# A fused attention and MLP kernel: first weight chunk in fp32, one tiled stretch per batch, second attention moved into the first MLP

## The chip, the core and the metric

The kernel runs on one core of one Trainium2 chip. The metric is device time in microseconds (us) of one execution. Every time below is from runs at a mean granted TensorE clock of 0.98 to 1.00, unless said otherwise. Engines: PE is TensorE (matmuls), PEld its weight loads, DVE is VectorE, ACT is ScalarE, POOL is GpSimd, SP is SyncE, which here only issues DMAs.

## The reference, cut to what matters

```python
# x: [8, 8, 512, 64] (batch, head, token, d); state: [8, 8, 32, 64]
xread = softmax(x @ state.T / 8) @ state        # 512 rows of a head
sread = softmax(state @ x.T / 8) @ x            # 32 rows of a head
y = concat([xread, sread], axis=2)              # heads are laid side by side: [8*544, 512]
out = silu(y @ w_in) @ w_out                    # w_in [512, 2048], w_out [2048, 512]
```

The kernel never forms `xread`. For each batch it multiplies the state into `w_in` first and calls the result `W1` (256 x 2048); then `silu(a @ W1) @ w_out` is the MLP of that batch's 512 xread rows, with `a` the normalised attention. The sread rows of all batches make one last small MLP.

## The kernel before

Work of PE, per batch: `g1(b, ft)` is two matmuls of 128x512 and a SILU on ACT, for 16 values of ft; `g2(b, tt, ft)` is one matmul of 128x512, 64 of them. I call these 96 matmuls per batch the wide ones. PE further does the transposes `x_T`, `a_T`, the scores `sc`, the tiled matmuls `w1_m` that make W1, and the tiled `sread_m`.

```python
def w1_m(b, j, bks):                     # W1, one chunk of 512 columns: 8 matmuls in 8 tiles of the array
    for kt in range(KT):
        for half in range(2):
            nc.tensor.matmul(bank[bks[half]][ds(32 * kt, 32), :],
                sbd[ds(64 * half, 64), b, kt, half, :],
                w_in_sb[ds(64 * half, 64), kt, ds(512 * j, 512)],
                ..., tile_position=(64 * half, 32 * kt))

def g1(b, ft):
    bk = bank[f"h{hctr[0] % 2}"]         # only two banks, h0 and h1, in turn
    ...                                  # two matmuls W1 x aT into bk
    nc.scalar.activation(g[b % 2][:, ft, :], bk[:], func=SILU, bias=0.0)

def att_tail(fill, b, s, a0, sg, dg):    # a phase: 64 g2 matmuls of batch k, with work of batch k+1 filled in
    add(fill, s, L(exs, b), L(W1p, b, 0))                       # W1 chunks 0 and 1
    ...
    add(fill, s + 14, L(W1p, b, 1), L(sread_m, b, "a1"), L(sread_n, b, "a1"))   # chunks 2 and 3, sread
    ...
    for i in range(16):
        add(fill, sg + dg * i, L(g1, b, i))
```

(Cuts are marked with dots.) The start loads x of batch 0 and of batch 1 on SP's queue, does the attention of both, and only then makes the first W1 chunk and starts the first MLP; `warm` matmuls on zeros fill PE's gaps meanwhile (the granted clock was 1.00). The first MLP runs both batches' `g1` steps interleaved with batch 0's `g2` steps, four `g2` at a time (`G2`), while the weights still arrive in eight chunks, `wi` and `wo` 0 to 3. The kernel uses PSUM as eight banks of 128x512 fp32, named o0, o1, w0, w1, h0, h1, a0, a1.

The softmax here doesn't subtract the row's maximum and nothing guards it: scores larger than these inputs give would overflow.

Of the kernel before, what the change touches and what calls it, by code (L numbers as in the profile page):

```python
# [19 lines left out]
def kernel(  # L20
# [8 lines left out]
    nc = tc.nc  # L29
# [13 lines left out]
    st_f = [pers.tile([128, 128], FP32, name=f"st_f{i}") for i in range(2)]  # L43
    st_nat = pers.tile([128, B, 128], BF16, name="st_nat")
# [81 lines left out]

    def x_T(b, kt, bk):
        v = bf(bk).rearrange("p (k c t) -> p k c t", k=2, c=4)
        for c in range(4):
            nc.tensor.transpose(  # L130
                v[:, kt % 2, c, :], x_n[b % 2][:, kt, c, ds(2, 128)], ident[:]
            )
# [14 lines left out]
    def x_Td(b):  # L147
        nc.sync.dma_start_transpose(
            xT[b % 2][:].rearrange("p k c t -> p (k c) t"),
            x_u[:].rearrange("p k c h d -> p (k c h d)"),  # L150
        )
        nc.vector.tensor_copy(
            x_n[b % 2][:, :, :, ds(2, 128)].rearrange("p k c e -> p (k c) e"),
            x_u[:].rearrange("p k c h d -> p (k c) (h d)"),
        )
# [28 lines left out]
    def norm_m(b, eng, kt=0, n=4):  # L184
        e = nc.vector if eng == "dve" else nc.gpsimd
        e.tensor_tensor(  # L186
            an[b % 2][:, :, :, ds(kt, n), :].rearrange("p h c k s -> p (h c) k s"),
            en[b % 2][:, :, :, ds(kt, n), :].rearrange("p h c k s -> p (h c) k s"),
            rs[b % 2][:, :, :, ds(kt, n)]
            .rearrange("p h c k -> p (h c) k")  # L190
            .unsqueeze(3)
            .to_broadcast([128, 8, n, NS]),
            op=MULT,
        )
# [53 lines left out]
    def w1_m(b, j, bks):  # L248
        for kt in range(KT):
            for half in range(2):  # L250
                nc.tensor.matmul(  # L251
                    bank[bks[half]][ds(32 * kt, 32), :],
                    sbd[ds(64 * half, 64), b, kt, half, :],
                    w_in_sb[ds(64 * half, 64), kt, ds(512 * j, 512)],
                    start=True,
                    stop=True,
                    skip_group_check=True,
                    tile_position=(64 * half, 32 * kt),
                )
# [66 lines left out]
    with tc.manual_schedule():  # L326
# [4 lines left out]
        for kt in range(KT):  # L331
            if kt == 2:
                nc.sync.dma_start(st_f[1][:], state[1].rearrange("h ns d -> ns h d"))
            load_x(1, nc.sync, kt, 1)
# [4 lines left out]
        make_identity(nc, ident[:])  # L339
# [7 lines left out]
        OB = XB  # L347
# [11 lines left out]
        def exs(b):  # L359
            for q in range(2):  # L360
                ex(b, 2 * q, 2, AB[q])
# [6 lines left out]
        cast_x(0, "dve", (0,))  # L368
        cp("pool", st_nat[:, 0, :], st_f[0][:])
        x_T(0, 0, XB[0])  # L370
        x_Te(0, 0, 1, XB[0], "act")
        cast_x(0, "dve", (1,))
        st_T(0, "a1", "act", "dve")
        cast_x(0, "dve", (2,), (0,))
        cast_x(0, "pool", (2,), (1,))
        cast_x(0, "dve", (3,), (0,))
        cast_x(0, "pool", (3,), (1,))
        cast_x(1, "pool", (0,), (1,))
        load_wi(0)
        load_wo(0)  # L380
        warm(8, "w1")
        x_T(0, 1, XB[1])
        x_Te(0, 1, 1, XB[1], "act")
        sc(0, 0, SB[0])
# [3 lines left out]
        x_Te(0, 2, 1, XB[2], "act")  # L388
        sc(0, 1, SB[1])
        ex(0, 1, 1, SB[1])  # L390
        warm(3, "w1")
        x_T(0, 3, XB[3])
        cast_x(1, "dve", (0,), (0,))
        x_Te(0, 3, 1, XB[3], "dve")
        warm(3, "o0")
# [3 lines left out]
        cast_x(1, "dve", (1,))  # L399
        cast_x(1, "act", (2,))  # L400
        norm_s(0, 0, 2)
        norm_m(0, "pool", 0, 2)
        x_T(1, 0, "o0")
        x_T(1, 1, "o0")
        x_Te(1, 0, 2, "o0", "dve")
        cp("act", st_nat[:, 1, :], st_f[1][:])
        cast_x(1, "act", (3,))
        warm(8, "a0")
        st_T(1, "a1", "dve", "dve")
        norm_s(0, 2, 2)  # L410
        norm_m(0, "pool", 2, 2)
        x_T(1, 2, "o1")
        x_T(1, 3, "o1")
        x_Te(1, 2, 2, "o1", "act")
        warm(4, "a0")
        sc(1, 0, "w0")
        sc(1, 1, "w0")
        ex(1, 0, 2, "w0")
        warm(8, "a0")
        sc(1, 2, "w1")  # L420
        sc(1, 3, "w1")
        ex(1, 2, 2, "w1")
        nc.scalar.preload_act_table(SILU)
        warm(8, "a0")
        a_T(0, (("a0", "dve"), ("a1", "dve")))
        W1x(0, 0, ("o0", "o1"), DA)
        load_wi(1)
        load_wo(1)
        load_wi(2)
        load_wo(2)  # L430
        norm_s(1, 0, 2)
# [3 lines left out]
        warm(6, "o0")  # L435


        g1(0, 0)
        g1(0, 1)
        sread_m(0, "a0")  # L440
        sread_n(0, "a0")
        g1(0, 2)
        g1(0, 3)
        load_wi(3)
        load_wo(3)
        load_x(2, nc.gpsimd)
        for b in range(2, B):
            load_st(b)
        G2(0, 0)
        sread_t(0, "a0", "dve")  # L450
        sread_m(1, "a1")
        sread_n(1, "a1")
        G2(0, 1)
        sread_t(1, "a1", "dve")
        a_T(1, (("a0", "dve"),))
        G2(0, 2)
        W1x(0, 1, AB, DA)
        G2(0, 3)
        W1x(1, 0, AB, DA)
        for j in (1, 2, 3):  # L460
            n = 3 * j - 3
            g1(0, 4 * j)
            g1(1, n)
            W1x(1, j, AB, DA)
            g1(0, 4 * j + 1)
            g1(0, 4 * j + 2)
            G2(0, 4 * j)
            g1(0, 4 * j + 3)
            G2(0, 4 * j + 1)
            g1(1, n + 1)  # L470
            if j == 3:
                cast_xu(2, "dve", (0, 1))
                cast_xu(2, "pool", (2, 3))
                x_Td(2)
                st_T(2, "a0", "dve", "dve")
            G2(0, 4 * j + 2)
            if j < 3:
                W1x(0, j + 1, AB, DA)
            g1(1, n + 2)
            G2(0, 4 * j + 3)  # L480
# [3 lines left out]
        g1(1, 9)  # L484


        WP = (("w0", "w1"), ("h0", "h1"))

        def W1p(b, i):
            for j in range(2):  # L490
                w1_m(b, 2 * i + j, WP[j])
            for j in range(2):
                w1_e(b, 2 * i + j, WP[j], DD if j == 0 else ("act", "act"))

        def phase(k, fill):
            for tt in range(4):
                bk = ("o0", "o1")[tt % 2]
                for ft in range(16):
                    g2(k, tt, ft, bk)
                    for f in fill.get(16 * tt + ft, ()):  # L500
                        f()
                o_e(k, tt, bk)

        def add(fill, step, *fs):
            fill.setdefault(int(step), []).extend(fs)
# [4 lines left out]
        def att_head(fill, b, s0, s1):  # L510
            add(fill, s0, L(st_T, b, "a0", "dve", "dve"))
            add(fill, s0, L(x_Td, b))
            if 4 < b + 1 < B:
                add(fill, s0, L(load_x, b + 1, nc.sync))
            add(fill, s1, L(scs, b, 0))
            add(fill, s1 + 2, L(scs, b, 1))

        def att_tail(fill, b, s, a0, sg, dg):
            add(fill, s, L(exs, b), L(W1p, b, 0))
            add(fill, s, L(norm_s, b, 0, 2), L(norm_m, b, "pool", 0, 2))  # L520
            add(fill, s, L(norm_s, b, 2, 2), L(norm_m, b, "dve", 2, 2))
            add(fill, s, L(nc.scalar.preload_act_table, SILU))
            add(fill, s + 14, L(W1p, b, 1), L(sread_m, b, "a1"), L(sread_n, b, "a1"))
            if b == 2:
                add(fill, a0, L(a_T, b, (("a0", "act"),)))
            else:
                add(fill, s, L(a_Td, b))
            add(fill, a0 + 2, L(sread_t, b, "a1", "dve"))
            for i in range(16):
                add(fill, sg + dg * i, L(g1, b, i))  # L530

        fill = {}
        for i in range(10, 16):
            add(fill, i - 10, L(g1, 1, i))
        add(fill, 2, L(scs, 2, 0))
        add(fill, 3, L(scs, 2, 1))
        att_tail(fill, 2, 6, 30, 35, 1.8)
        add(fill, 6, L(cast_xu, 3), L(load_x, 4, nc.sync))
        att_head(fill, 3, 37, 58)
        phase(1, fill)  # L540

        for k in range(2, 7):
            fill = {}
            att_tail(fill, k + 1, 0, 24, 35, 1.8)
            if k + 2 < B:
                add(fill, 0, L(cast_xu, k + 2))
                att_head(fill, k + 2, 34, 56)
            phase(k, fill)


        fill = {}
        for i in range(16):
            add(fill, 2 + 3 * i, L(g1, 8, i))
        phase(7, fill)
# [5 lines left out]
        for i, cols in enumerate(((0, 256), (256, 512))):  # L560
            for ft in range(16):
                g2(8, 1, ft, ("o1", "w0")[i], cols)
            o_e(8, 1, ("o1", "w0")[i], "dve" if i else "act", nc.sync if i else nc.scalar, cols)
# [30 lines left out]
```

## Time and profile before

| | before |
|---|---|
| time, median of the first 3 runs | 221.55 us (221.09 to 221.85) |
| span of the profiled run | 219.7 us |
| PE busy | 209.2 us, 95% |
| first wide matmul | 15.89 us in the records, in fact 15.68 (below) |
| one phase in the middle | 23.15 us |

From the page of the kernel before: busy time and share of the span of each engine, the row of PE in 40 slices (in tenths), and the chain of waits by engine.

```profile
PE 209.2 (95%) x1652; PEld 104.2 (47%) x1678; DVE 84.0 (38%) x171; ACT 131.5 (60%) x221; POOL 40.7 (19%) x78
PE   7779999999999999999999999999999999999993
...
PE 90%; DMA 2%; SPq 2%; issue 1%; ACT 1%; DVE 1%; POOL 0%
```

PE bounds the kernel, except in the first three slices. The timeline of PE, kernel before, shows the end of that start (columns: start, length, engine, line, operation, tiles, shapes, count, idle time before and what ended it).

```profile
12.67 0.61 PE L321 MATMUL ps_a<-zeros 128*128 128x128 bf16 x8
13.50 0.62 PE L202 MATMUL ps_a<-ident,an 128*128 128x128 bf16 x8 [0.22 <-POOL an L186]
14.05 0.41 PE L251 MATMUL ps_o<-w_in_sb,sbd 64*32 64x512 bf16 x8
15.34 0.49 PE L321 MATMUL ps_o<-zeros 128*128 128x128 bf16 x6 [0.88 <-DVE W L79]
15.89 0.81 PE L272 MATMUL ps_h<-aT,W 128*128 128x512 bf16 x3
```

The transposes of the attention wait for POOL's normalisation, then come the first W1 group (L251), its eviction by DVE, and the first `g1`. A record is missing here: `g1(0, 0)` and `g1(0, 1)` are four wide matmuls, and the view has three. The trace has the weight loads of all four, the first at 15.62, when the last of the six `warm` matmuls starts (they are 0.055 us apart), so the first wide matmul was at about 15.68. The run e8b_old_start (below), which has the same start and no record missing here, shows four, the first 0.06 us after the last `warm`:

```profile
15.78 0.49 PE L323 MATMUL ps_o<-zeros 128*128 128x128 bf16 x6 [0.88 <-DVE W L79]
16.11 1.03 PE L274 MATMUL ps_h<-aT,W 128*128 128x512 bf16 x4
```

The next lines, from the view of the kernel before, are one phase's two tiled stretches.

```profile
95.75 0.59 PE L296 MATMUL ps_o<-w_out_sb,g 128*128 128x512 bf16 x2
96.28 0.41 PE L251 MATMUL ps_w<-w_in_sb,sbd 64*32 64x512 bf16 x8
96.50 0.56 PE L251 MATMUL ps_h<-w_in_sb,sbd 64*32 64x512 bf16 x8
97.23 2.97 PE L296 MATMUL ps_o<-w_out_sb,g 128*128 128x512 bf16 x13 [0.16 <-issue]
100.13 0.41 PE L251 MATMUL ps_w<-w_in_sb,sbd 64*32 64x512 bf16 x8
100.35 0.40 PE L251 MATMUL ps_h<-w_in_sb,sbd 64*32 64x512 bf16 x8
100.68 0.43 PE L218 MATMUL ps_a<-x_n,en 128*32 128x65 bf16 x32
101.27 2.54 PE L296 MATMUL ps_o<-w_out_sb,g 128*128 128x512 bf16 x11 [0.16 <-issue]
```

Two things have to be known to read this. Wide matmuls start 0.216 us apart when nothing holds them, though each is shown with 0.38 us: they are pipelined. (The Trainium skill, "TensorE: Matmul & The Clock Gate", Back-to-back issue gap, gives N / 2.4 + 2.5 ns for a single warm matmul, which is 0.216 us for 512 columns; this trace has it. The same section puts a sustained stream of such matmuls, each with its weight load, at about 0.131 us; this trace does not agree, since its streams of them keep 0.216, and the measurement decides.) And the program has 14 wide matmuls between the two stretches where the trace has 13: the one right after a stretch is missing in the records, which is what "idle 0.16" stands for. So the first stretch lasts from 96.18 (95.75 and two matmuls) to 97.02, 0.84 us, and the second from 100.03 to 101.05, 1.02 us.

### The profile page before, as it was taken

Reading aid. Unit: us, or ns where it says so; the run is one execution under the profiler, and the core shown is the slowest. Engines: PE = TensorE matmul, PEld = TensorE weight load, DVE = VectorE, ACT = ScalarE, POOL = GpSimd, SP = SyncE. Lnnn points to the kernel's source line nnn. Section 1 sums busy time; section 2 is a strip of 40 time slices with the busy share of each in tenths; the row PEclk is TensorE's granted clock in tenths of the full one; section 3 lists DMA queues with packets and bytes.
Section 4 is the critical chain, followed back from the end, with each engine's and each line's share of the span. In section 5 each row is a group of like instructions: output and inputs, shape, how many; then the busy total and the mean of one; then the engine's idle time right before and its main releaser. Section 6 shows DMA issues by size and latency. Waiting matters only on the chain.

```text
span 219.7 us, 4129 instructions
## 1 busy us (share of the span) xinstructions
PE 209.2 (95%) x1652; PEld 104.2 (47%) x1678; DVE 84.0 (38%) x171; ACT 131.5 (60%) x221; POOL 40.7 (19%) x78
## 2 busy tenths in 40 slices
PE   7779999999999999999999999999999999999993
PEld 7555334453544444444444444444443444566552
DVE  4767321445730672139312841087107600111110
ACT  3873766669677846776477837692669277433210
POOL 1778222001600070007000610043001000000000
PEclk9999999999999999999999999999999999999999
DMA  6899999289551138512770269015411311111112
GB/s 204 229 179 169 206 232 188 42 225 286 191 120 51 48 97 189 196 48 51 187 243 3 69 169 276 16 51 145 95 48 51 97 48 51 49 48 48 51 48 96
DMA packets 36868, 26.56 MB, mean 121 GB/s; under 512 B 20848, under 2 KB 32368, under 8 KB 36848
## 3 DMA queue, kind: packets, MB, share of 16 engines
q1 hardware_dynamic: 30160, 20.39, 32.8%
q0 software_dynamic: 6128, 5.44, 14.8%
q10 hardware_dynamic: 560, 0.46, 0.6%
q8 instruction: 13, 0.21, 0.4%
q14 instruction: 7, 0.06, 0.1%
HBM read 17.30 MB, written 8.91 MB: 119 GB/s over the span
## 4 chain that ended last, share of the span: by engine, by line
PE 90%; DMA 2%; SPq 2%; issue 1%; ACT 1%; DVE 1%; POOL 0%
PE ps_o L296 49%; PE ps_h L272 25%; PE ps_w L296 4%; PE ps_h L283 3%; DMA x_f<-in_x_dram 2%; PE ps_w L251 2%; PE ps_h L251 2%; PE ps_a L218 1%; SPq L91 1%; PE ps_a L160 1%; PE ps_a L251 1%; ACT x_n L83 1%; PE ps_a L202 1%; DVE W L79 1%; POOL an L186 0%
## 5 line engine op out<-in xcount | busy, mean ns | idle before, releaser
L296 PE MATMUL ps_o<-w_out_sb,g 128*128 128x512 bf16 x462 | 124.8, 379 | 2.3 <-issue 1.7
L280 ACT ACTIVATE g<-ps_h 128x512 bf16<-128x512 f32 x128 | 75.7, 598 | 51.9 <-PE ps_h L272 49.6
L272 PE MATMUL ps_h<-aT,W 128*128 128x512 bf16 x248 | 73.6, 379 | 0.5 <-DVE W L79 0.3
L296 PEld LDWEIGHTS <-g 128*128 128x128 bf16 x512 | 47.9, 98 | 51.8 <-issue 1.6
L79 DVE COPY o_sb<-ps_o 128x512 f32<-128x512 f32 x30 | 20.6, 689 | 91.7 <-PE ps_o L296 76.7
L272 PEld LDWEIGHTS <-W 128*128 128x128 bf16 x256 | 24.3, 98 | 29.7 <-issue 1.6
L186 POOL TENSOR_TENSOR an<-en,rs 128x512 bf16<-128x512 bf16 x9 | 9.5, 1060 | 110.8 <-ACT W L83 56.6
L81 POOL CAST x_u<-x_f 128x256 bf16<-128x256 f32 x44 | 17.8, 447 | 4.5 <-DMA x_f<-in_x_dram 4.5
L79 DVE CAST W<-ps_w 128x512 bf16<-128x512 f32 x24 | 15.3, 679 | 3.5 <-PE ps_w L251 3.5
L83 ACT ACTIVATE W<-ps_h 128x512 bf16<-128x512 f32 x24 | 13.1, 603 | 0.1
L291 ACT ACTIVATE g_s<-ps_h 128x256 bf16<-128x256 f32 x16 | 6.1, 383 | 11.2 <-PE ps_h L283 11.2
L181 DVE TENSOR_REDUCE rs<-en 128x16 f32<-128x512 bf16 x16 | 10.5, 659 | 3.2 <-ACT en L171 3.1
L79 DVE CAST W<-ps_a 128x512 bf16<-128x512 f32 x7 | 4.8, 691 | 14.2 <-PE ps_a L251 14.2
L283 PE MATMUL ps_h<-xsT,w_in_sb 128*128 128x256 bf16 x64 | 9.6, 273 | 0.0
L296 PE MATMUL ps_w<-w_out_sb,g 128*128 128x512 bf16 x32 | 9.5, 379 | 0.1
L283 PEld LDWEIGHTS <-w_in_sb 128*128 128x128 bf16 x64 | 6.3, 98 | 4.1
L160 PEld LDWEIGHTS <-xT 128*128 128x128 bf16 x128 | 5.9, 98 | 4.3 <-DVE xT L79 0.4
L251 PEld LDWEIGHTS <-sbd 64*32 64x32 bf16 x256 | 3.1, 88 | 9.9 <-issue 9.4
L508 ACT ACT_TABLE_LOAD x6 | 7.7, 1283 | 0.1
L171 ACT ACT_TABLE_LOAD x6 | 7.7, 1283 | 0.1
L321 PEld LDWEIGHTS <-zeros 128*128 128x128 bf16 x86 | 6.6, 116 | 2.3 <-DVE zeros L335 1.2
L171 ACT ACTIVATE en<-ps_a 128x512 bf16<-128x512 f32 (+1 forms) x14 | 7.3, 564 | 0.4 <-PE ps_a L160 0.2
(66 smaller groups left out, 126.7 us busy)
## 6 DMA issues: line engine op xcount, KB each, us to landing
out_dram<-o_sb SPq DMA_DIRECT2D x32, 256.0 KB, 2.3
x_f<-in_x_dram SPq DMA_DIRECT2D x5, 1024.0 KB, 6.7
x_f<-in_x_dram SPq DMA_DIRECT2D x8, 256.0 KB, 4.5
w_in_sb<-in_moe_w_in_dram POOLq DMA_DIRECT2D x4, 512.0 KB, 9.6
w_out_sb<-in_moe_w_out_dram POOLq DMA_DIRECT2D x4, 512.0 KB, 11.9
x_f<-in_x_dram POOLq DMA_DIRECT2D x1, 1024.0 KB, 18.1
out_dram<-o_sb ACTq DMA_DIRECT2D x1, 256.0 KB, 2.5
st_nat<-in_state_dram POOLq DMA_DIRECT2D x6, 32.0 KB, 13.1
```

The source lines that it names most:

```text
L79: nc.vector.tensor_copy(dst, src)
L81: nc.gpsimd.tensor_copy(dst, src)
L83: nc.scalar.activation(dst, src, func=COPY, bias=0.0)
L160: nc.tensor.matmul(v[:, kt % 2, :, c, :], xT[b % 2][:, kt, c, :], sbd[:, b, kt, :, :], start=True, stop=True, skip_group_check=True,)
L171: nc.scalar.activation(en[b % 2][:, :, :, ds(kt, n), :].rearrange("p h c k s -> p k (h c) s"), v[:, ds(kt % 2, n)], func=EXP, bias=0.0, sc ...
L181: nc.vector.tensor_reduce(v, en[b % 2][:, :, :, ds(kt, n), :], axis=AX, op=ADD)
L186: e.tensor_tensor(an[b % 2][:, :, :, ds(kt, n), :].rearrange("p h c k s -> p (h c) k s"), en[b % 2][:, :, :, ds(kt, n), :].rearrange("p h ...
L251: nc.tensor.matmul(bank[bks[half]][ds(32 * kt, 32), :], sbd[ds(64 * half, 64), b, kt, half, :], w_in_sb[ds(64 * half, 64), kt, ds(512 * j, ...
L272: nc.tensor.matmul(bk[:], W1[b % 2][:, half, ds(128 * ft, 128)], aT[b % 2][:, half, :, :], start=(half == 0), stop=(half == 1), skip_group ...
L280: nc.scalar.activation(g[b % 2][:, ft, :], bk[:], func=SILU, bias=0.0)
L283: nc.tensor.matmul(bk[:, 0:256], w_in_sb[:, kt, ds(128 * ft, 128)], xsT[:, kt, :, :, :], start=(kt == 0), stop=(kt == KT - 1), skip_group_ ...
L296: nc.tensor.matmul(bank[bk][:, c0:c1], src[:, ft, ds(128 * tt, 128)], w_out_sb[:, ft, c0:c1], start=(ft == 0), stop=(ft == 15), skip_group ...
```

## The change

The intent is to start the first MLP earlier and to leave tiled mode less often. The first W1 chunk's `w_in` columns come uncast, on SP's queue right behind batch 0's x, and are multiplied in fp32, so that the chunk need not wait for POOL's casting queue. Batch 1's load and attention move out of the start into the first MLP. In the phases, all four W1 groups of a batch and its sread come in one tiled stretch. The core of the diff, cut:

```diff
+    def st_f32(bk, e0, e1): ...          # the state of batch 0, in fp32
+    w_f = x_f[1][:].rearrange("p k h e -> p k (h e)")
+    def w1f_m(bks): ...                  # as w1_m, from sbd_f and w_f, both fp32
 # start
-        for kt in range(KT):
-            ...
-            load_x(1, nc.sync, kt, 1)
+        nc.sync.dma_start(st_f[1][:], state[1].rearrange("h ns d -> ns h d"))
+        nc.sync.dma_start(w_f, win_re[:, :, 0:512])
...
-        W1x(0, 0, ("o0", "o1"), DA)
+        w1f_m(("w0", "w1"))
+        w1_e(0, 0, ("w0", "w1"), ("act", "act"))
...
+        for kt in range(KT):
+            cp("pool", w_in_sb[:, kt, 0:512], w_f[:, kt, :])
+        load_x(1, nc.gpsimd, 0, 2)
+        load_x(1, nc.gpsimd, 2, 2)
 # first MLP: batch 1's transposes, scores and softmax between batch 0's steps
+        xTs(1, 0, "dve")
+        G2(0, 5)
+        xTs(1, 1, "dve")
+        G2(0, 6)
+        scs(1, 0)
+        scs(1, 1)
+        exs(1)
...
 # phases
+        def tiled(b, tt):
+            cur, nxt, third, srb = (TB[(tt + i) % 4] for i in range(4))
+            bks = ((srb, nxt), HB, AB, (third, cur))
+            for j in range(4):
+                w1_m(b, j, bks[j])
+            w1_e(b, 0, bks[0], DA)
+            sread_m(b, srb)
+            for j in range(1, 4):
+                w1_e(b, j, bks[j], ("act", "dve"))
+            sread_n(b, srb)
```

Smaller parts: the phases' outputs rotate over four banks instead of two, the transposed attention of the third batch comes by a DMA transpose instead of eight PE transposes, and the last output piece is cut into two of 128 columns.

## The prediction

> **What bounds the kernel now.** TensorE (PE): busy 209.2 of 219.7 us (95%, the page's first part), 90% of the chain of waits, granted clock 1.00. Only the start is not bound by PE: the PE timeline shows the first MLP matmul at 15.89 us. The chain there runs through the second batch's load (lands 9.33), its casts on ACT, its transposes, exponentials, the normalisation on POOL (to 13.45) and the evictions of aT and W1 (to 15.3). After that a phase takes 23.15 us: 96 wide matmuls at 0.216 us (20.7), 0.47 for scores, and two tiled stretches of 0.84 and 1.02 us (from last wide matmul to next, corrected for missing records).
>
> **What the change does.**
>
> 1. Start. The second batch leaves the start; the first W1 chunk comes uncast by the first queue and is multiplied in fp32. The first batch's scores ended at about 8.4 us; exponential 0.38, reduction, reciprocal and half-size normalisation about 1.2 bring it to about 10.2. The 1 MB fp32 chunk is queued where the second batch's loads were (landing 9.33), but shares the engines with two weight chunks issued earlier: I estimate 10.3 to 11.3. The Trainium skill, "FP8 and Floating Point Precision", TensorE Precision Notes, says true fp32 takes 4 passes. A tiled bf16 group of 8 costs 0.22 us, so I estimate 0.9 us if the tiles still overlap (no run here shows it; fully serial about 7). Then two evictions in a row on ACT (2 x 0.6). First MLP matmul at about 13.2 us: gain 2.7.
>
> 2. The second attention moves into PE's full stretch: 17 transposes at 0.055 and 16 scores, +1.4 us. Two table loads (1.28 each) and a row of DVE work (two W1 evictions 1.36, reductions, normalisation) come between: I estimate +1.0 us of PE waits around the third chunk of batch 0. Fewer lone tiled stretches in the first MLP (7 to 5, about 0.22 of overhead each): -0.4. Old waits there: -0.3.
>
> 3. One tiled stretch per batch, not two, for six batches. Lower limit: enter 0.1, four groups 0.87, switch 0.11, sread 0.37: 1.45 against 1.86. The Trainium skill, "TensorEngine Tiling (Array Packing)", Key Properties, says that a change of tiling mode drains TensorE; the trace agrees, with gaps of 0.1 to 0.16 us at each change. But sread now waits for DVE's eviction of its bank (0.68 us after the first group) and the last group for ACT's output copy (0.6): about 1.65. Gain 0.2 to 0.4 each, 1.5 in all.
>
> 4. Tail: 128-column last pieces, -0.2.
>
> Weights should stay just ahead: a chunk lands every 2.5 us in the saturated part (DMA share above 1.1 from 11 to 37 us).
>
> **Prediction.** 221.55 - 2.7 + 1.4 + 1.0 - 0.7 - 1.5 - 0.2 = about 218.8 us; 8 in 10: 216.6 to 221.3. Faster by over 2%: 0.18; within 2%: 0.79; slower: 0.03.
>
> **What would show it.** First MLP matmul near 13.2 us, released by the fp32 chunk rather than by attention; the fp32 group near 0.9 us; one tiled stretch of 1.5 to 1.7 us per batch, a phase of about 22.9; PE waits on DVE's W1 copies in 22 to 28 us; PE's idle smaller by about 2 us.
>
> **What would make it wrong.** Fp32 tiles that don't overlap (first MLP matmul 3 to 6 us later); the fp32 chunk landing past 12 us; POOL's casts of that chunk (4 of about 0.9 us) delaying the later loads until PE waits for weights; the tiled stretch waiting on evictions until it is no shorter than both old ones; or a quicker start and no waits in the first MLP, which would take it past 2%.

## The result

| | before | after |
|---|---|---|
| time, median of 4 runs each | 221.34 us | 220.38 us (220.20 to 220.76) |
| ratio, 95% interval | | 0.9956 (0.9932 to 0.9981) |
| span of the profiled run | 219.7 us | 218.7 us |
| first wide matmul | 15.68 us (15.89 in the records) | 13.55 us |
| PE busy | 209.2 us | 211.2 us |

Ratios here and below are the mean time of one kernel's fast runs over the mean of the other's fast runs of the same rounds, so not quite the ratio of the medians that are quoted. The time lies in the predicted range, but the gain is 0.44% where 1.2% was forecast.

From the page of the changed kernel, the same three lines:

```profile
PE 211.2 (97%) x1664; PEld 104.5 (48%) x1664; DVE 81.9 (37%) x172; ACT 134.3 (61%) x224; POOL 44.9 (21%) x85
PE   7789999999999999999999999999999999999993
...
PE 86%; DMA 4%; ACT 3%; DVE 2%; issue 2%; SPq 1%; ACTq 0%; DVEq 0%
```

PE's idle time went from 10.5 to 7.5 us, three times as much as the span lost. The rest is in what counts as busy. The timeline of PE, changed kernel, at the start:

```profile
8.80 1.46 PE L348 MATMUL ps_o<-zeros 128*128 128x512 bf16 x6
11.61 1.09 PE L278 MATMUL ps_w<-x_f,sbd_f 64*32 64x512 f32 x16 [1.35 <-DMA x_f<-in_moe_w_in_dram]
12.64 0.62 PE L214 MATMUL ps_a<-ident,an 128*128 128x128 bf16 x8
13.09 0.59 PE L348 MATMUL ps_h<-zeros 128*128 128x512 bf16 x2
13.55 1.23 PE L299 MATMUL ps_h<-aT,W 128*128 128x512 bf16 x4
```

The first MLP starts 2.13 us earlier (2.34 by the records), and it is the fp32 chunk (landing at 11.57) that releases it. The fp32 group takes 1.03 us to the next matmul. So the start did what it was meant to do. Now three places of the first MLP, same view:

```profile
26.62 0.59 PE L323 MATMUL ps_o<-w_out_sb,g 128*128 128x512 bf16 x2
27.13 0.39 PE L299 MATMUL ps_h<-aT,W 128*128 128x512 bf16 x1
27.73 0.82 PE L299 MATMUL ps_h<-aT,W 128*128 128x512 bf16 x3 [0.21 <-DVE W L80]
...
33.83 0.59 PE L323 MATMUL ps_o<-w_out_sb,g 128*128 128x512 bf16 x2
34.33 1.87 PE L299 MATMUL ps_h<-aT,W 128*128 128x512 bf16 x6
36.22 0.60 PE L323 MATMUL ps_w<-w_out_sb,g 128*128 128x512 bf16 x2
...
38.62 1.03 PE L299 MATMUL ps_h<-aT,W 128*128 128x512 bf16 x4
39.90 0.59 PE L299 MATMUL ps_h<-aT,W 128*128 128x512 bf16 x2 [0.25 <-ACT g L307]
```

Six wide matmuls that start 0.216 us apart take 1.30 us; from 34.33 to 36.22 they took 1.89, and the two before 34.33 took 0.50 instead of 0.43: 0.66 us of waits, of which the view calls nothing idle, because each matmul is drawn 0.38 us long and a wait of up to 0.16 us hides in that. (The Trainium skill, "Perfetto Trace Analysis", Per-engine timelines, says that TensorE's end times are estimated from the instruction's size, not observed; the trace fits, with every wide matmul drawn 0.376 to 0.390 us long, however long the next had to wait.) At 27 us the wait is 0.46, at 39.90 it is 0.42, both by the same reckoning. So waits of PE are best taken from starts: start to start, less 0.216.

One tiled stretch of the changed kernel, same view:

```profile
95.52 3.62 PE L323 MATMUL ps_w<-w_out_sb,g 128*128 128x512 bf16 x16
99.06 0.41 PE L263 MATMUL ps_o<-w_in_sb,sbd 64*32 64x512 bf16 x8
99.29 0.40 PE L263 MATMUL ps_h<-w_in_sb,sbd 64*32 64x512 bf16 x8
99.50 0.40 PE L263 MATMUL ps_a<-w_in_sb,sbd 64*32 64x512 bf16 x8
99.72 0.50 PE L263 MATMUL ps_w<-w_in_sb,sbd 64*32 64x512 bf16 x8
100.28 0.43 PE L230 MATMUL ps_o<-x_n,en 128*32 128x65 bf16 x32
100.64 3.41 PE L323 MATMUL ps_o<-w_out_sb,g 128*128 128x512 bf16 x15
```

From 98.97 (95.52 and 16 matmuls) to 100.64 is 1.67 us, against 0.84 and 1.02 before. (The other stretches: 1.76, 1.67, 1.87, 1.67 and 1.67.) The Trainium skill, "TensorEngine Tiling (Array Packing)", Key Properties, says that a change of tiling mode drains TensorE; this trace agrees, with 0.09 us from the last wide matmul to the first tiled one; worked out from starts, the gaps at a change that nothing else delays are 0.09 to 0.11 us in both traces.

Going through both traces start by start, I get this account of the spans. Each row is a sum of start-to-start times; the row of waits is what wide matmuls took beyond 0.216 us, where that was over 0.02 us. Missing records are filled in from the weight loads.

| part | before, us | after, us | change | the prediction's figure |
|---|---|---|---|---|
| to the first wide matmul | 15.68 | 13.55 | -2.13 | -2.7 |
| second attention on PE within the MLPs | 0 | 1.42 | +1.42 | +1.4 |
| eight PE transposes of the third batch | 0.45 | 0 | -0.45 | not seen |
| W1 groups in the first MLP | 3.05 | 2.70 | -0.35 | -0.4 |
| waits between wide matmuls | 0.64 | 2.22 | +1.6 | +1.0 - 0.3 |
| tiled stretches of six batches | 11.22 | 10.32 | -0.90 | -1.5 |
| after the last `g2` of the batches | 10.83 | 10.67 | -0.16 | -0.2 |
| sum | | | -1.0 | -2.7 |

The spans differ by 0.93. This account is one profiled run of each kernel, and an account is not a proof; the experiments test its rows.

### The profile page after: what moved, and what is told of

Its sections match the earlier page's. It is cut to its first block, busy times and chain, and to the rows that moved or that the text cites. A ratio compares the mean times of both kernels' runs of the same rounds, so it can differ in the third digit from the quotient of the medians.

```text
span 218.7 us, 4106 instructions
## 1 busy us (share of the span) xinstructions
PE 211.2 (97%) x1664; PEld 104.5 (48%) x1664; DVE 81.9 (37%) x172; ACT 134.3 (61%) x224; POOL 44.9 (21%) x85
## 4 chain that ended last, share of the span: by engine, by line
PE 86%; DMA 4%; ACT 3%; DVE 2%; issue 2%; SPq 1%; ACTq 0%; DVEq 0%
PE ps_o L323 26%; PE ps_h L299 25%; PE ps_w L323 24%; DMA x_f<-in_moe_w_in_dram 4%; PE ps_h L310 3%; PE ps_a L172 1%; PE ps_a L263 1%; DVE W L80 1%; SPq L92 1%; ACT en L183 1%; PE ps_o L230 1%; PE ps_h L263 1%; PE ps_w L263 1%; PE ps_o L263 1%; ACT L568 1%
## 5 line engine op out<-in xcount | busy, mean ns | idle before, releaser
L299 PE MATMUL ps_h<-aT,W 128*128 128x512 bf16 x256 | 75.4, 379 | 0.6 <-ACT g L307 0.3
L323 PE MATMUL ps_w<-w_out_sb,g 128*128 128x512 bf16 x256 | 73.1, 379 | 0.0
L323 PE MATMUL ps_o<-w_out_sb,g 128*128 128x512 bf16 x256 | 66.0, 379 | 0.0
L198 POOL TENSOR_TENSOR an<-en,rs 128x512 bf16<-128x512 bf16 (+1 forms) x9 | 9.2, 1027 | 114.3 <-ACT en L183 72.2
L80 DVE COPY o_sb<-ps_w 128x512 f32<-128x512 f32 (+1 forms) x13 | 8.5, 659 | 52.6 <-PE ps_w L323 52.5
L80 DVE COPY o_sb<-ps_o 128x512 f32<-128x512 f32 x14 | 9.5, 687 | 29.8 <-PE ps_o L323 29.7
L84 ACT ACTIVATE o_sb<-ps_o 128x512 f32<-128x512 f32 (+1 forms) x4 | 2.2, 544 | 10.9 <-PE ps_o L323 8.1
L84 ACT ACTIVATE o_sb<-ps_w 128x512 f32<-128x512 f32 (+1 forms) x5 | 2.7, 533 | 8.5 <-issue 6.9
L80 DVE CAST W<-ps_h 128x512 bf16<-128x512 f32 x10 | 6.7, 683 | 2.8 <-PE ps_h L263 2.8
L80 DVE COPY sbd<-ps_a 64x128 bf16<-64x128 bf16 x15 | 4.3, 288 | 8.2 <-PE ps_a L120 7.1
```

What stands on the lines that cost most here:

```text
L80: nc.vector.tensor_copy(dst, src)
L198: e.tensor_tensor(an[b % 2][:, ds(h0, hn), :, ds(kt, n), :].rearrange("p h c k s -> p (h c) k s"), en[b % 2][:, ds(h0, hn), :, ds(kt, n), ...
L299: nc.tensor.matmul(bk[:], W1[b % 2][:, half, ds(128 * ft, 128)], aT[b % 2][:, half, :, :], start=(half == 0), stop=(half == 1), skip_group ...
L323: nc.tensor.matmul(bank[bk][:, c0:c1], src[:, ft, ds(128 * tt, 128)], w_out_sb[:, ft, c0:c1], start=(ft == 0), stop=(ft == 15), skip_group ...
```

## The experiments

My theory: the start's gain of 2.13 us is repaid inside the first MLP, by attention moved onto a busy PE and by waits for evictions and for the two h banks; the phases gain, but less than thought, as the one stretch waits for evictions. The main rival: the weights' landing sets the pace of the first MLP, so that an earlier start can only wait. Each kernel ran 4 to 6 times, in rounds with the kernel before; all ratios are to before. The changed kernel was not run again in these sets, which were on chips 10, 6, 9 and 11: it is compared with them by its ratio, 0.9956, alone. One execution of e5_bf16_first and one of the kernel before in the last set (278.27 us at clock 0.755) are left out of the ratios.

### The two halves of the change apart

The new start and first MLP with the old phases, then the old start and first MLP with the new phases (e1_two_stretches keeps the last output piece cut in two):

```diff
 # e1_two_stretches, on the changed kernel
-        def tiled(b, tt): ...            # and the plan of the new phases
+        WP, W1p, phase, att_head, att_tail as before
+        att_tail(fill, 2, 10, 34, 38, 1.6)      # the first phase, shifted to fit the new first MLP
 # e2_stretch_alone, on the kernel before
-        WP, W1p, phase, att_head, att_tail
+        def tiled(b, tt): ...            # and the plan of the new phases
```

> The changed kernel's start and first MLP, with the old phases (two tiled stretches per batch, PE transposes of the second phase's attention): part 3 undone. My account of the two traces says that the new phases save 0.90 us in the tiled stretches of six batches (11.22 to 10.32) and 0.45 in eight transposes that became a DMA, so this kernel should take about 1.35 us more than the changed one: about 221.7, ratio to before about 1.002. Rival: the phases gained nothing, since a phase takes 23.13 against 23.15 us in the middle of the trace; then it takes 220.4 as the changed one.

> The old start and the old first MLP, with the new phases (one tiled stretch per batch): part 3 alone. By the same account it takes about 1.35 us less than before: 220.0, ratio about 0.994, which would be all of the gain of the whole change and more. Rival (the gain of the whole is the start's): no faster than before.

Measured: e1_two_stretches 222.26 us, ratio 1.003 (1.001 to 1.005). e2_stretch_alone 220.22 us, ratio 0.9943 (0.9917 to 0.9968). Both are as the account says, and the rivals fall: the phases alone gain about 1.3 us (0.57%), and the start with its first MLP alone costs about 0.7 (0.3%). A start that is over 2 us quicker, with the work that it moves into the first MLP, makes the whole kernel slightly slower.

### What bounds the start

Two edits of the start, on the changed kernel:

```diff
 # e4_late_weights
-        load_wo(0)        # after x's second piece
-        load_wi(1)        # after x's fourth piece
         norm_m(0, "pool", 2, 2, 1, 1)
+        load_wo(0)
+        load_wi(1)
 # e5_bf16_first
-        nc.sync.dma_start(w_f, win_re[:, :, 0:512])
+        load_wi(0)                        # POOL's first DMA, cast to bf16
-        st_f32("a1", "dve", "dve")
-        w1f_m(("w0", "w1"))
+        w1_m(0, 0, ("w0", "w1"))
-        for kt in range(KT):
-            cp("pool", w_in_sb[:, kt, 0:512], w_f[:, kt, :])
```

> The changed kernel, with the two weight chunks that POOL issues at 5.0 and 7.5 us issued only after its normalisation (about 11 us). Theory: the fp32 chunk landed at 11.57 only because those two share the 16 DMA engines; alone it lands at about 9.9, where the last of the same bytes landed before, and the first MLP matmul comes about 12.5 (then limited by POOL's normalisation to 11.1), 1.0 us earlier; the weights then land later, and PE waits for them in the first MLP, which may eat it. Rival: the queue itself is slow for this chunk; it lands at 11.5 as before.

> The changed kernel, but the first W1 chunk comes as the first DMA of POOL, cast to bf16 on the way, and is multiplied in bf16 (no fp32 matmuls, no POOL casts of it, no fp32 copies of the state). Theory: the start's limit in the changed kernel is the fp32 chunk (landing 11.57, 1.09 us of matmuls); here the chunk is there before 10 us, attention is the limit, and the first MLP matmul comes at about 12.3 instead of 13.55, total about 219.3. Rival: the chunk's transfer delays the first batch's x by about 1.5 us, so the first MLP matmul is at 13.5 or later and the total no better than 220.4.

e4_late_weights: 223.09 us, ratio 1.0063 (1.0046 to 1.0079). The chunk landed at 11.17 instead of 11.57, not at 9.9, so the theory that the two weight chunks hold it up by 1.5 us falls; and since the landing scatters more than 0.4 us from profile to profile (below), not even that is shown to be theirs. What the edit cost shows in PE's timeline:

```profile
14.68 1.04 PE L299 MATMUL ps_h<-aT,W 128*128 128x512 bf16 x3
16.86 0.59 PE L323 MATMUL ps_w<-w_out_sb,g 128*128 128x512 bf16 x2 [1.14 <-DMA w_out_sb<-in_moe_w_out_dram]
...
19.38 0.41 PE L263 MATMUL ps_a<-w_in_sb,sbd 64*32 64x512 bf16 x8 [0.53 <-DMA w_in_sb<-in_moe_w_in_dram]
```

This is what a first MLP that waits for weights looks like: the wait names the DMA. The changed kernel's waits in its first MLP name DVE and ACT.

e5_bf16_first: 223.85 us (median of the five fast runs), ratio 1.0097 (1.0064 to 1.013). The rival holds, and by more than it said. The chunk as POOL's first DMA slows x: its last piece lands at 10.64 instead of 6.94, and PE stands still for it.

```profile
10.25 0.61 PE L140 MATMUL ps_w<-ident,x_n 128*128 128x128 bf16 x4 [3.20 <-POOL x_n L82]
...
17.03 1.14 PE L299 MATMUL ps_h<-aT,W 128*128 128x512 bf16 x4
```

The first wide matmul is at 17.03, later than before the change. Not all of that is x's: PE's granted clock was 0.5 from 9.44 to 16.27 us of this run, from before that wait's end on, so the matmuls of the start took longer too (the fast runs of this kernel all have a mean clock of 0.982 to 0.992); how much each did was not tested. So in this start the order on the first queue, x and then the fp32 chunk behind it, is what lets the chunk come early without delaying x; the price is 1.03 us of fp32 matmuls instead of 0.22.

### The waits in the first MLP

The same work and the same loads, in another order and with the banks of two W1 groups exchanged. `G2(b, ft, t0, t1)` is the part t0 to t1 of a step of four `g2`.

```diff
 # e3_no_back_to_back, on the changed kernel
-        G2(0, 6)
         scs(1, 0)
-        scs(1, 1)
-        exs(1)
+        ex(1, 0, 2, "a0")
+        W1x(0, 2, HB, DD)
+        G2(0, 6, 0, 2)
+        scs(1, 1)
+        ex(1, 2, 2, "a1")
         nc.scalar.preload_act_table(SILU)
-        W1x(0, 2, HB, DD)
+        G2(0, 6, 2, 4)
...
-        G2(0, 10)
-        w1_m(0, 3, AB)
-        W1x(1, 1, HB, DA)
-        w1_e(0, 3, AB, DA)
-        G2(0, 11)
-        g1(1, 0)
-        g1(0, 12)
+        G2(0, 10, 0, 2)
+        w1_m(0, 3, HB)
+        w1_m(1, 1, AB)
+        w1_e(0, 3, HB, DA)
+        w1_e(1, 1, AB, DA)
+        G2(0, 10, 2, 4)
+        G2(0, 11, 0, 2)
+        g1(0, 12)
+        G2(0, 11, 2, 4)
+        g1(1, 0)
         g1(0, 13)
...                                       # and the same around G2(0, 12), G2(0, 13), g1(0, 14)
```

> The changed kernel with the first MLP put in another order, same work and same loads: the third W1 chunk is multiplied before the second half of the scores, and halves of second-matmul steps are held back so that no three first-matmul steps follow one another. Theory: the PE waits of the changed kernel in its first MLP (0.46 us at 27 us, 0.66 at 34 to 36, 0.42 at 39.9) are waits for evictions and for the two h banks that SILU on ACT turns round in about 1.28 us; they go, about 1.3 us less than the changed kernel: 219.1, ratio to before about 0.990. Rival: the weights' landing sets the pace of the first MLP (a chunk lands every 2.5 us until 32 us), so the waits only change into waits for DMA and the time stays at 220.4.

Measured: 219.24 us, ratio 0.9898 (0.9884 to 0.9913), against 0.9956: the intervals do not meet, and the size is what the theory said. PE's timeline of this kernel where the first wait of the three was, and where one is left:

```profile
26.16 0.59 PE L323 MATMUL ps_o<-w_out_sb,g 128*128 128x512 bf16 x2
26.59 1.03 PE L299 MATMUL ps_h<-aT,W 128*128 128x512 bf16 x4
27.55 0.41 PE L263 MATMUL ps_a<-w_in_sb,sbd 64*32 64x512 bf16 x8
...
37.66 0.59 PE L323 MATMUL ps_o<-w_out_sb,g 128*128 128x512 bf16 x2
38.53 1.02 PE L299 MATMUL ps_h<-aT,W 128*128 128x512 bf16 x4 [0.28 <-DVE W L80]
```

The four `g1` matmuls after 26.59 run through without a wait, where 0.46 us was lost; no wait turned into one for a weight chunk. That refutes the rival for this kernel: the weights were there, though not by much (the third `w_in` chunk landed at 24.01, and its first W1 group started at 24.27). Part of the trace's gain is not the waits', though. In the two profiled runs the time from the first wide matmul to the last MLP fell by only 0.53 us, because the waits between wide matmuls fell by 1.16 but three tiled stretches of the first MLP, which now wait for a bank or for SILU, became longer by about 0.65 in all; another 0.47 came from the chunk landing at 11.10 in this run instead of 11.57. The timed runs show the sum of these, and how much of the 1.3 us belongs to the order alone stays uncertain by about that 0.5.

### The tiled stretch

Here sread comes first, and the last W1 group takes its bank and the bank of the output just copied, so that both are free by then:

```diff
 # e6_sread_first, on the changed kernel
-            bks = ((srb, nxt), HB, AB, (third, cur))
+            bks = ((third, nxt), HB, AB, (srb, cur))
+            sread_m(b, srb)
             for j in range(4):
                 w1_m(b, j, bks[j])
-            w1_e(b, 0, bks[0], DA)
-            sread_m(b, srb)
-            for j in range(1, 4):
-                w1_e(b, j, bks[j], ("act", "dve"))
             sread_n(b, srb)
+            for j in range(4):
+                w1_e(b, j, bks[j], DA if j == 0 else ("act", "dve"))
 # e6b_sread_first: sread_n directly after sread_m
```

> The changed kernel with the tiled stretch in another order: sread first, then the four W1 groups, the last of them in sread's bank and in the bank of the output just copied. Theory: the stretch of 1.67 us holds about 0.1 us of wait for ACT's output copy and 0.12 for DVE's eviction of sread's bank; without them it is about 1.5, six times 0.17 less: 219.4, ratio about 0.991. Rival: the stretch is set by the eviction of the next output's bank, and stays at 1.67.

> Both of the last two edits. If both theories hold and the gains add: about 218.1 us, ratio about 0.984.

> The old start and first MLP with the new phases and sread first in the tiled stretch. The run with the old start and the new phases took 0.9943 of before; 6 times 0.17 us less would be about 0.990. Told against the run with both edits it says whether the new start is worth having once its waits are gone: theory says it is, by about 0.6 us (start 2.34 earlier, tail 0.17 less, fewer stretches 0.35, against 1.42 of attention moved in and what is left of the waits).

These three gave wrong results (relative error 66260), by my mistake: `sread_n` was issued after the group that overwrites its bank, so it normalised W1 values. Their times (219.78 us, ratio 0.9909; 218.66, 0.9862; 219.67, 0.9908) are of kernels that do not compute the reference, and I use them for nothing (only the landings of their fp32 chunk, which come before the mistake, are counted below). Mended, they ran again:

> As the run with sread first that gave a wrong result, mended: sread's normalisation is now issued before the W1 group that overwrites its bank, so that group waits for it. Theory: the stretch shrinks from 1.67 to about 1.55 us (the wrong one had 1.58 to 1.64), six times about 0.1 us: 219.6, ratio about 0.992. Rival: the last group now waits for the normalisation on DVE and nothing is gained (0.9956).

> The reordered first MLP and sread first, mended. If the gains add (0.0058 by reordering, 0.003 to 0.004 by sread first): ratio about 0.986, 218.5 us.

> The old start and first MLP with the new phases and sread first, mended: ratio about 0.991. If the run with both edits on the new start is faster than this one by about 0.5%, the new start pays once its waits are gone; if they are equal, the start's gain is only the moved-in attention's cost, whatever the order.

e6b_sread_first: 219.95 us, ratio 0.9928 (0.9909 to 0.9947), where the changed kernel has 0.9956; the intervals overlap, so the timed runs alone do not settle it. The profile does: the six stretches take 9.77 us together instead of 10.32 (1.61 for most, 1.67 before). PE's timeline of e6b_sread_first:

```profile
122.69 0.40 PE L263 MATMUL ps_h<-w_in_sb,sbd 64*32 64x512 bf16 x8
122.90 0.40 PE L263 MATMUL ps_a<-w_in_sb,sbd 64*32 64x512 bf16 x8
...
123.17 0.39 PE L263 MATMUL ps_w<-w_in_sb,sbd 64*32 64x512 bf16 x1
123.61 0.59 PE L323 MATMUL ps_o<-w_out_sb,g 128*128 128x512 bf16 x2
```

The groups follow each other nearly without a wait now, but from the last of them to the next wide matmul there are 0.44 us. In the first MLP of the kernel before, where no bank held it up, a group and the change of mode after it took 0.34 (21.58 to 21.92), so about 0.1 us of it is a wait: that matmul's bank has to be evicted by ACT (until 123.57), which does the output's copy first. So both the theory and the rival of the first expectation were right in part: two waits went, and a third took over most of their room.

e7b_both: 218.81 us, ratio 0.9879 (0.9860 to 0.9899). Subtracting both single gains from 0.9956 gives 0.987, so they add. Against e6b_sread_first, which ran in the same rounds and differs by the order alone, it gains 0.0049 (1.1 us), and these intervals do not meet: that is the cleanest test of the order, although its chunk landed earlier in the profiled run (11.28 against 11.63). e8b_old_start, which has the old start and first MLP: 219.67 us, ratio 0.9913 (0.9895 to 0.9931). Now the new start is worth about 0.3% (0.9879 against 0.9913; the intervals overlap by 0.0004), where with the waits still in it (0.9956 against e2_stretch_alone's 0.9943) it was worth nothing that could be told.

### A version that beats both, and the landing of the fp32 chunk

In e3_no_back_to_back the wait at 38.53 is on DVE's W1 copy, and DVE was late because casts of the third batch's x stood in front of it, waiting 1.63 us for their load (landing at 35.4). e9_best moves these casts behind the copies and splits two more back-to-back pairs:

```diff
 # e9_best, on e7b_both
-        cast_xu(2, "dve", (0, 1))
         cast_xu(2, "pool", (2, 3))
-        x_Td(2)
-        x_nu(2)
...
         w1_e(1, 2, AB, DA)
+        cast_xu(2, "dve", (0, 1))
+        x_Td(2)
+        x_nu(2)
...                                       # and G2(0, 9), G2(0, 15) in halves with g1 between
 # e10_split_chunk on the changed kernel, e11_best_split on e9_best
-        nc.sync.dma_start(w_f, win_re[:, :, 0:512])
+        for kt in range(KT):
+            nc.sync.dma_start(w_f[:, kt, :], win_re[:, kt, 0:512])
```

> As both, and in the first MLP the casts of the third batch's x, which made DVE wait 1.6 us for their load (landing 35.4) in front of two W1 evictions, now come after these, and two more back-to-back pairs are split. The profile of the reordered run still had 0.44 us of PE wait on DVE's W1 copy at 38.5, 0.33 in the stretch at 31.6 and 0.2 at 43.3; at most 0.9 us less than both: about 217.7, ratio 0.983. Rival: the first MLP is then bound by the weights' landing and stays where it is (0.986).

> The changed kernel with the fp32 chunk loaded in four DMAs of 256 KB, as x is. If one large load is the cause of the late tail, all four land by about 10 us and the first MLP matmul is at about 12.2 us, about 1 us less in the start; some of it comes back as waits in the first MLP; ratio 0.992 to 0.994. Rival: the tail belongs to slow DMA engines, not to the load's size; the last of the four lands at 11 us or later and the ratio stays at 0.9956.

> The best version (reordered first MLP, sread first) with the chunk in four loads: if the theory holds the start no longer varies between runs, ratio about 0.983; else 0.985 as without.

e9_best: 218.28 us, ratio 0.9850 (0.9829 to 0.9870), the best of the one-load kernels, 2.1 us less than the changed kernel by the medians of their own sets. That its edit gained over e7b_both is not shown. The intervals overlap, and in the profiles the time from the first wide matmul to the last MLP is no shorter, 193.30 against 193.18 us, while the fp32 chunk happened to land at 10.07 against 11.28. The waits at 38.5 and 43.3 are gone, but PE now waits for a weight chunk, the third of `w_in` (landing at 23.92):

```profile
23.01 0.40 PE L172 MATMUL ps_a<-sbd,xT 128*128 128x64 bf16 x8
23.96 0.41 PE L263 MATMUL ps_h<-w_in_sb,sbd 64*32 64x512 bf16 x8 [0.55 <-DMA w_in_sb<-in_moe_w_in_dram]
```

So in this profile the rival holds in part: with the other waits gone and an early start, the weights set the pace at one place, by about 0.6 us. (In e7b_both the same group waited 0.2 us, for a landing at 24.62.)

e10_split_chunk: 219.35 us, ratio 0.9894 (0.9880 to 0.9908), well below 0.9956. The last of the four loads landed at 10.57, the first wide matmul was at 12.51, and from there to the last MLP it took 194.38 us against 194.52: the start's gain went straight through, none was eaten by weights. That speaks against the weights as the limit of the changed kernel a second time. But e11_best_split is at 218.22 us, ratio 0.9844 (0.9830 to 0.9858), no clear gain over e9_best, and in its profile the last piece landed at 11.41. With one load, the profiles of kernels that are the same up to there have landings of 11.57, 11.10, 11.10, 9.51, 11.81, 11.63, 11.28 and 10.07. So one load or four does not explain the scatter, and what does stays open.

## Why the prediction was wrong

The time lay in the range; the gain was 0.96 us by the medians where 2.75 us was forecast. Point by point:

- **Start, "First MLP matmul at about 13.2 us: gain 2.7".** Right in kind and nearly in size: 13.55 us, gain 2.13, released by the fp32 chunk as said. Of what is missing, 0.2 us is the record that was missing before (15.68, not 15.89), and 0.35 is the later first matmul. The fp32 tiles overlap: 1.03 us where 0.9 was estimated. The landing, "10.3 to 11.3", was 11.57 in this run, and the reason given, sharing with two weight chunks, found no support: with those issued later it was 11.17, within the scatter of the landing.
- **"The second attention moves into PE's full stretch ... +1.4 us".** Right: 1.42. Overlooked was that the third batch's transposes left PE in the same change, -0.45.
- **"I estimate +1.0 us of PE waits around the third chunk of batch 0 ... Old waits there: -0.3".** This is the step that failed most. The waits grew by 1.6 us net, not 0.7. Around the third chunk it was only 0.46; the rest sits at 34 to 36 us (0.66), 39.9 (0.42), 44.3 (0.20), at 13.96 (0.19, for the second of ACT's two evictions) and in smaller pieces, where I had looked for none. At 34 to 36 and 39.9 three `g1` steps stand in a row, with ACT just done with evictions (34.63) or turning the banks round. A bank of the two is free again 1.28 us after its first matmul started (38.62 to 39.90), and two `g1` steps of 0.43 us do not fill that. Reordering took the ratio from 0.9956 to 0.9898, and from 0.9928 to 0.9879 within the same rounds.
- **"Gain 0.2 to 0.4 each, 1.5 in all" for the tiled stretch.** The mechanism and the length were right (1.65 foreseen, 1.67 in most stretches), but 1.86 less 1.65 is 0.2, not the middle of "0.2 to 0.4": the sum took a mean that its own estimate did not support. Measured: 0.90 for six, 0.15 each, with two stretches at 1.76 and 1.87.
- **"Weights should stay just ahead".** Right for this kernel: no wait of its first MLP names a weight chunk, and e3_no_back_to_back and e10_split_chunk gained without new ones. How just it was shows in e9_best, where PE waits 0.6 us for one.
- **Tail, -0.2.** Right: -0.16.
- **"PE's idle smaller by about 2 us"** as a sign was of little use: idle fell by 3.0 us and the span by 0.9, since short waits between matmuls count as busy.

With 0.6 too much at the start, 0.9 too little for waits and 0.6 too much for the stretches, less the 0.45 overlooked, the forecast sum of -2.7 becomes about the measured -1.0.

## What to carry to other kernels

Starting the bound engine earlier is worth only what the work moved behind the start does not cost there: price that work, and then look, step by step, whether the longer queue still alternates between work that another engine must clear (here SILU on two banks, 1.28 us) and work that needs nobody. Take PE's waits from start-to-start times, not from idle shares, and count the records against the program: one missing at the start was worth 0.21 us here. When a change merges stretches, list what each matmul in the merged one waits for, bank by bank; removing one wait tends to show the next.

## What the Trainium skill lacked or had wrong

- "TensorEngine Tiling (Array Packing)" does not say whether fp32 matmuls overlap in tiles. They do here: eight of 64x32 tiles with 512 columns appear as 16 records, about 7 ns apart within each of two rounds that start 0.45 us apart, 1.03 us in all to the next matmul. That fits the four passes of "FP8 and Floating Point Precision", TensorE Precision Notes, at about 0.2 us each; that a round is two passes is not shown.
- "DMA: Bandwidth & Descriptors", Latency and other measured facts, gives a first byte of about 1 us for GpSimd's path. In the changed kernel, with SP's queue full, the weight chunk that POOL issued at 5.03 us has its first packets in the trace after 8.5 us. In e5_bf16_first, where it was issued at 1.25, its packets mix with x's from 3.5 us on and x's last piece lands 3.7 us later. Why the first packets came after 3.5 us in the one case and 2.2 us in the other was not tested.
- No page says how much the landing of one 1 MB load scatters: 9.51 to 11.81 us over eight profiled runs with the same instructions before it. In the changed kernel's trace the queue's traffic falls to about a quarter after 9.5 us; why was not found.
- "Perfetto Trace Analysis" says that TensorE's ends are estimates, but not how much wait this can hide: up to 0.16 us before each matmul of 512 columns, 0.66 us in one place of this trace with no idle time shown.
- "TensorE: Matmul & The Clock Gate", Back-to-back issue gap, has about 131 ns for a matmul of 512 columns in a sustained stream; in these traces, with a weight load for each, it is 216 ns.
